# Folding the second batch's keys three slots later, with two issue points per slot, and building one expert's weight forms a step later

## The chip, the cores and the metric

The kernel runs on one core of a Trainium2 chip. The metric is device time in microseconds (us), the median of several executions. PE is the matrix engine (TensorE), DVE the vector engine, ACT the scalar engine, Pool the engine that issues the casting loads, SP the one that issues stores and DMA transposes. Differences here are below one per cent, so every kernel of the experiments was timed in five rounds beside the kernel before, unless a section says "one look": a single profiled execution.

## The reference, cut to what matters

```
attention, B = 8, H = 8, S = 576, D = 64:
  k_p, v_p = means of k and v over 8 neighbouring rows          # 72 rows a head
  attn = softmax(q k_p^T / sqrt(D));   x = attn v_p
mixture of E = 4 experts over N = 4608 tokens, width 512, hidden 1024:
  out = sum_e p[:, e] * (relu(x w1[e]) w2[e])                   # p: normalised domain_probs
```

## The kernel before

The tokens form nine chunks of 512: one for each batch, and a last one from the 64 left-over rows of each. A *step* is one chunk and one expert: step `s` multiplies by w1 ("up", with ReLU) for its own chunk and expert and by w2 ("down") for those of step `s - 1`. A step has eight *slots*. Steps 0 to 3 are chunk 0 (batch 0), so step 4 needs the attention of batch 1. While steps 2 and 3 run, that attention is threaded between the matmuls by a table of slots:

```python
        return {                                          # second_attention(), before
            19: [lambda: fold_keys(1, lo), lambda: fold_keys(1, hi)],   # DVE
            20: [second_keys],                            # PE transposes, ACT copy
            21: [lambda: second_queries(0)],              # PE transposes, DVE copy
            22: [lambda: second_queries(1)],
            23: [lambda: scores(1, 0)],                   # PE, then exp on ACT
            24: [lambda: scores(1, 1), lambda: fold_values(1, lo)],
            25: [lambda: scores(1, 2), lambda: fold_values(1, hi)],
            26: [lambda: scores(1, 3)],
            27: [lambda: context(1, 0), lambda: turn(1, 0)],   # PE, divide on DVE, DMA transpose
            ...                                           # 28, 29, 30: contexts 1, 2, 3
            31: [loads, lambda: load_v(2), lambda: combine_x(1)],
        }
```

`second_keys`, `second_queries`, `scores` and `context` all use one PSUM tile of two banks, one at a time. `combine_x` builds the *x forms* on DVE, sums of blocks of the transposed x; step 4's third product needs them. A step's up part is two rounds of seven products of blocks, with down matmuls between them:

```python
        product(c, e, j, 1, g, True)      # 4 matmuls of 256 columns each
        r1 = keep(g)                      # ACT
        between(0)                        # 3 down matmuls (512 columns), then the slot's pieces
        product(c, e, j, 2, s, True)
        relu_sum(top[:, :, 0:TH], s, r1)  # DVE
        product(c, e, j, 6, g, False)
        r2 = keep(g)
        between(1)                        # 4 down matmuls
        ...                               # products 5 and 7, r3, a relu_sum
        between(2)                        # 5 down matmuls
        product(c, e, j, 4, g, False)
        ...
        between(3)                        # 4 down matmuls
        product(c, e, j, 3, d, False)
        relu_sum(top[:, :, TH:NT], d, r2)
```

The w1 blocks need four sums for each expert too (*weight forms*, `combine_w1`, four DVE operations, one to a slot). All casting loads go through one queue in this order:

```python
        load_probs()
        load_w1(1)
        load_w1(2)
        load_w2(1)
        load_w1(3)
        load_k(1)
        load_q(1)
        load_v(1)
        load_w2(2)       # w2 of the third expert: first used by step 3's down matmuls
        load_w2(3)
        ...
```

Loads for batch 2 follow in the same queue. Pool runs nothing else, so each is issued as soon as its buffer is free: q once the query transposes are done, v once the folds of the values are done.

The softmax here doesn't subtract the row's maximum and nothing guards it: scores larger than these inputs give would overflow.

## Time and profile before

| | before |
|---|---|
| median time | 539.47 us (538.76 to 540.0, 3 runs) |
| span of the profiled execution | 538.1 us |
| PE busy | 516.0 us, 96% |
| DVE, ACT busy | 58%, 43% |

PE is the bound, and the change removes no work from it. So only its waits matter. The longest by the view of PE's waits (what waited, for whom: total us, times, longest us):

```profile
PE g_ps L569 <- DVE H_sb L622: 6.0, 9, 0.8
PE kpt_ps L272 <- DVE kp L190: 4.8, 2, 3.7
PE g_ps L569 <- DVE xf L558: 1.8, 1, 1.8
...
PE o_ps L653 <- DMA w_bf<-in_moe_w_dram: 0.6, 1, 0.6
PE two L348 <- DVE x_tok L330: 0.5, 1, 0.5
...
PE two L225 <- DVE qT L286: 0.4, 1, 0.4
```

The second line is the wait for batch 1's folded keys. Here is PE's timeline around it (start us, us, engine, line, operation, tiles, shapes, count, idle time before and who ended it). `kpt_ps` are the key transposes, `o_ps` the down matmuls, `g_ps` the products:

```profile
47.99 0.81 PE L653 MATMUL o_ps<-w_bf,H_sb 128*128 128x512 bf16 x3
52.49 0.42 PE L272 MATMUL kpt_ps<-ident,kp 72*128 72x72 bf16 x4 [3.68 <-DVE kp L190]
54.07 0.42 PE L272 MATMUL kpt_ps<-ident,kp 72*128 72x72 bf16 x4 [1.16 <-DVE kp L190]
...
63.81 0.81 PE L653 MATMUL o_ps<-w_bf,H_sb 128*128 128x512 bf16 x3
...
82.90 0.61 PE L569 MATMUL g_ps<-xf,w_bf 128*128 128x256 bf16 x4 [1.76 <-DVE xf L558]
```

The line at 63.81 is step 3's first down matmul, the first use of the third expert's w2. It did not wait: that load was issued at 41.73 and took 18.9 us to land, so it was there at 60.6. DVE began the folds at 50.76, after 2.00 us of waiting for the load of k.

The long wait costs twice. The table by stretches shows the granted clock in the third column from the right (the first two columns are the stretch and its length):

```profile
48.00:53.00 5.00, 1.23 (x9) 0.44 (x6) 2.94 (x7) 0.59 (x1) 0.00 (x0) 0.82 1.36 198
53.00:58.00 5.00, 3.93 (x19) 2.29 (x20) 3.43 (x8) 1.22 (x2) 0.00 (x0) 0.50 1.24 206
58.00:63.00 5.00, 4.57 (x42) 3.01 (x40) 3.71 (x6) 1.18 (x2) 1.84 (x3) 1.00 1.26 194
```

By the clock records of the trace PE had half its clock from 51.17 to 57.99. I call this a half-clock stretch.

### The profile page before, as it was taken

The numbers are of one execution on the slowest core, as the hardware profiler recorded it, in microseconds if no ns is written. First come the engines' busy times: TensorE is split into PE (matmuls) and PEld (weight loads), VectorE is DVE, ScalarE is ACT, GpSimd is POOL, SyncE is SP. The second block draws the span as 40 slices with busy tenths as digits, with TensorE's granted clock in tenths as the row PEclk, the third lists the DMA queues.
The fourth block names the chain that finished last, engine by engine and source line by source line (L and its number), as shares of the span: only waits on it lengthen the run. The fifth ranks groups of instructions, "written<-read, shape, count | busy, mean of one in ns | idle before, by whom it ended". The sixth has DMA issues, their size and how long they took to land.

```text
span 538.1 us, 9237 instructions
## 1 busy us (share of the span) xinstructions
PE 516.0 (96%) x3811; PEld 330.2 (61%) x3811; DVE 310.0 (58%) x560; ACT 230.5 (43%) x371; POOL 46.8 (9%) x66
## 2 busy tenths in 40 slices
PE   8896998899999999999999998999999999999996
PEld 4743565566656666566666665666566666666663
DVE  2435785746854667367826656469456644654454
ACT  3652443463355334633473335533643345334430
POOL 8352100200100000101100002000000000000000
PEclk9999899999999999999999999999999999999999
DMA  9999992943580205916631029331101110011003
GB/s 136 203 204 201 193 125 68 158 65 72 77 155 10 41 12 129 133 30 94 113 68 31 20 66 173 45 68 52 40 12 29 49 42 1 10 40 40 2 0 79
DMA packets 75130, 41.52 MB, mean 77 GB/s; under 512 B 44480, under 2 KB 70464, under 8 KB 75088
## 3 DMA queue, kind: packets, MB, share of 16 engines
q0 software_dynamic: 33744, 22.63, 29.4%
q1 hardware_dynamic: 41344, 18.29, 14.3%
q8 instruction: 30, 0.49, 0.4%
q14 instruction: 12, 0.10, 0.1%
HBM read 45.16 MB, written 9.44 MB: 101 GB/s over the span
## 4 chain that ended last, share of the span: by engine, by line
PE 78%; DVE 10%; DMA 8%; POOL 1%; ACT 1%; issue 1%; DVEq 0%; POOLq 0%
PE o_ps L653 39%; PE g_ps L569 36%; DMA w_bf<-in_moe_w_dram 4%; DMA kraw<-in_k_dram 3%; DVE H_sb L622 2%; DVE acc L667 2%; PE two L225 2%; PE two L348 1%; DVE kraw L181 1%; DVE kp L190 1%; ACT r L618 1%; DVE kraw L183 1%; DVE vraw L181 1%; POOL w_bf L134 1%; DVE vraw L183 0%
## 5 line engine op out<-in xcount | busy, mean ns | idle before, releaser
L653 PE MATMUL o_ps<-w_bf,H_sb 128*128 128x512 bf16 x1152 | 294.4, 380 | 0.6 <-DMA w_bf<-in_moe_w_dram 0.6
L569 PEld LDWEIGHTS <-w_bf 128*128 128x128 bf16 x1904 | 181.5, 98 | 79.8 <-issue 13.6
L622 DVE CUSTOM_DVE_ANT_0 H_sb<-g_ps,r 128x512 bf16<-128x512 f32 x204 | 139.7, 688 | 155.8 <-ACT r L618 88.4
L618 ACT COPY r<-g_ps 128x512 f32<-128x512 f32 x204 | 119.4, 585 | 203.1 <-PE g_ps L569 203.1
L653 PEld LDWEIGHTS <-H_sb 128*128 128x128 bf16 x1152 | 112.9, 98 | 78.6 <-issue 1.3
L569 PE MATMUL g_ps<-xf,w_bf 128*128 128x256 bf16 x1088 | 152.7, 273 | 6.2 <-DVE H_sb L622 4.4
L569 PE MATMUL g_ps<-xT,w_bf 128*128 128x256 bf16 x720 | 99.0, 274 | 1.6 <-DVE H_sb L622 1.6
L667 DVE SCALAR_TENSOR_TENSOR acc<-o_ps,p_all,acc 128x512 f32<-128x512 f32 x108 | 80.5, 745 | 19.6 <-PE o_ps L653 19.6
L639 ACT ACTIVATE H_sb<-g_ps 128x512 bf16<-128x512 f32 x68 | 40.4, 595 | 50.6 <-PE g_ps L569 50.6
L229 ACT ACTIVATE expT<-two 72x1024 bf16<-72x1024 f32 x28 | 28.5, 1018 | 10.7 <-PE two L225 10.7
L664 ACT ACTIVATE acc<-o_ps,p_all 128x512 f32<-128x512 f32 x36 | 24.8, 689 | 6.2 <-PE o_ps L653 6.2
L100 POOL DMA_DIRECT2D q_sb<-in_q_dram x7 | 6.3, 897 | 233.9 <-DMA qT<-q_sb 219.1
L330 DVE TENSOR_TENSOR x_tok<-two,inv 128x512 bf16<-128x512 f32 x32 | 22.1, 692 | 1.1
L348 PEld LDWEIGHTS <-expT 72*128 72x128 bf16 x256 | 12.3, 98 | 8.4 <-DVE x_tok L330 1.0
L329 DVE RECIPROCAL inv<-two 128x8 f32<-128x8 f32 x32 | 6.5, 204 | 14.2 <-PE two L348 11.0
L569 PE MATMUL g_ps<-x_rem,w_bf 128*128 128x256 bf16 x96 | 13.3, 273 | 0.0
L348 PE MATMUL two<-vp,expT 72*128 72x65 bf16 x224 | 11.9, 194 | 0.5 <-DVE x_tok L330 0.5
L134 POOL DMA_DIRECT2D w_bf<-in_moe_w_dram x16 | 11.5, 726 | 9.3 <-DMA w_bf<-in_moe_w_dram 9.2
L225 PE MATMUL two<-qT,kpT 64*72 64x256 bf16 x112 | 11.5, 283 | 0.4 <-DVE qT L286 0.4
L225 PEld LDWEIGHTS <-kpT 64*72 64x72 bf16 x112 | 4.1, 107 | 12.3 <-issue 12.3
L181 DVE TENSOR_TENSOR kraw<-kraw 72x1024 bf16<-72x1024 bf16 x14 | 9.5, 678 | 2.0 <-DMA kraw<-in_k_dram 2.0
L181 DVE TENSOR_TENSOR vraw<-vraw 72x1024 bf16<-72x1024 bf16 x14 | 9.5, 678 | 0.0
(82 smaller groups left out, 172.7 us busy)
## 6 DMA issues: line engine op xcount, KB each, us to landing
out_dram<-acc SPq DMA_DIRECT2D x32, 256.0 KB, 2.4
w_bf<-in_moe_w_dram POOLq DMA_DIRECT2D x16, 256.0 KB, 9.9
w_bf<-in_moe_w_dram POOLq DMA_DIRECT2D x4, 1024.0 KB, 16.8
kraw<-in_k_dram POOLq DMA_DIRECT2D x7, 576.0 KB, 9.5
vraw<-in_v_dram POOLq DMA_DIRECT2D x7, 576.0 KB, 11.4
q_sb<-in_q_dram POOLq DMA_DIRECT2D x7, 512.0 KB, 6.2
out_dram<-acc SPq DMA_DIRECT2D x8, 128.0 KB, 2.3
H_sb<-in_k_dram POOLq DMA_DIRECT2D x2, 288.0 KB, 4.5
```

What stands on the lines that cost most here:

```text
L181: nc.vector.tensor_add(out=raw[:, hs, 0:4, :], in0=raw[:, hs, 0:4, :], in1=raw[:, hs, 4:8, :])
L225: nc.tensor.matmul(two[0:SP, r2].rearrange("j (h r p) -> j h r p", h=2, r=2)[:, hh], lhsT=kpT[lo:lo + D, h, 0:SP], rhs=qT[lo:lo + D, h],)
L229: nc.scalar.activation(out=state[("expT", b)][:, 2 * pair:2 * pair + 2].rearrange("j h r s p -> j s (h r) p"), in_=two[0:SP].rearrange("j ...
L330: nc.vector.tensor_tensor(out=x_tok[:], in0=c_ps[:, :, :, 0:D], in1=inv[:].unsqueeze(3).to_broadcast([P, 2, NPAIR, D]), op=ALU.mult,)
L348: nc.tensor.matmul(bank[:, i * (D + 1):(i + 1) * (D + 1)], lhsT=expT[:, h, r // 2, r % 2, :], rhs=vp[:, h, :],)
L569: nc.tensor.matmul(bank[:, t, :], lhsT=w1_bf[:, e, block, kc, lo:lo + P], rhs=x[:, kc, :], start=(first and t == 0 and kc == 0), stop=(t = ...
L618: nc.scalar.copy(out=r[:], in_=ps[:])
L622: nc.vector._custom_dve(TENSOR_ADD_SAT, out=out, in0=ps[:], in1=r[:], s0=BIG, s1=0.0)
L639: nc.scalar.activation(out=low[:, :, 0:TH], in_=g[:], func=ACT.Relu)
L653: nc.tensor.matmul(sums[r][:], lhsT=hidden[(c, e)][:, fc, r * P:(r + 1) * P], rhs=w2_bf[:, e, fc, :], start=(fc == 0), stop=(fc == FCH - 1),)
L664: nc.scalar.activation(out=accs[(c, r)][:], in_=o_ps[:], func=ACT.Copy, scale=prob)
L667: nc.vector.scalar_tensor_tensor(out=dst, in0=o_ps[:], scalar=prob, in1=dst, op0=ALU.mult, op1=ALU.add,)
```

## The change

The intent is to fold the keys when their load has landed, so that DVE does not stand and hold up PE, to place pieces more finely, and to take four weight forms out of the stretch where DVE is busiest. Now each `between` has two issue points, one before and one after its down matmuls, so point 44 is the start of slot 22 and point 47 the end of slot 23.

```diff
-            19: [lambda: fold_keys(1, lo), lambda: fold_keys(1, hi)],
-            20: [second_keys],
-            21: [lambda: second_queries(0)],
-            22: [lambda: second_queries(1)],
-            23: [lambda: scores(1, 0)],
-            24: [lambda: scores(1, 1), lambda: fold_values(1, lo)],
-            25: [lambda: scores(1, 2), lambda: fold_values(1, hi)],
-            26: [lambda: scores(1, 3)],
-            27: [lambda: context(1, 0), lambda: turn(1, 0)],
...                              # 28 to 30: contexts 1 to 3; 31: loads
+            44: [lambda: fold_keys(1, lo)],
+            46: [lambda: fold_keys(1, hi)],
+            47: [second_keys],
+            48: [lambda: second_queries(0)],
+            49: [lambda: second_queries(1)],
+            51: [lambda: scores(1, 0), lambda: fold_values(1, lo)],
+            53: [lambda: scores(1, 1)],
+            55: [lambda: scores(1, 2), lambda: fold_values(1, hi)],
+            57: [lambda: scores(1, 3)],
+            59: [lambda: context(1, 0), lambda: turn(1, 0)],
+            60: [lambda: context(1, 1), lambda: turn(1, 1)],
+            61: [lambda: context(1, 2), lambda: turn(1, 2)],
+            62: [lambda: context(1, 3), lambda: turn(1, 3)],
+            63: [loads, lambda: load_v(2), lambda: combine_x(1)],
...
             def between(j, n):
+                point()
                 if s > 0:
                     down(*steps[s - 1], j, n)
                 slot()          # calls point() too
...
-            elif s == 3:
+            elif s == 4:
                 forms_due.extend(combine_w1(1))
```

More of the change, by code (lines that the diff above doesn't have):

```diff
@@ L475, in second_attention @@
         return {
-            19: [lambda: fold_keys(1, lo), lambda: fold_keys(1, hi)],
-            20: [second_keys],
-            21: [lambda: second_queries(0)],
-            22: [lambda: second_queries(1)],
-            23: [lambda: scores(1, 0)],
-            24: [lambda: scores(1, 1), lambda: fold_values(1, lo)],
-            25: [lambda: scores(1, 2), lambda: fold_values(1, hi)],
-            26: [lambda: scores(1, 3)],
-            27: [lambda: context(1, 0), lambda: turn(1, 0)],
-            28: [lambda: context(1, 1), lambda: turn(1, 1)],
-            29: [lambda: context(1, 2), lambda: turn(1, 2)],
-            30: [lambda: context(1, 3), lambda: turn(1, 3)],
-            31: [loads, lambda: load_v(2), lambda: combine_x(1)],
+            44: [lambda: fold_keys(1, lo)],
[12 more added lines that the diff above has]
+            63: [loads, lambda: load_v(2), lambda: combine_x(1)],
         }
@@ L728, with point @@
         at = 0
-        def slot():
-            nonlocal due, at
-            if forms_due:
-                forms_due.popleft()()
+        def point():
+            nonlocal at
             for piece in placed.pop(at, ()):
@@ L736, in slot @@
             at += 1
+        def slot():
+            nonlocal due
+            if forms_due:
+                forms_due.popleft()()
+            point()
             due += per_slot
@@ L760, in between @@
             def between(j, n):
+                point()
                 if s > 0:
```

## The prediction

> **What bounds the kernel now.** TensorE. The page has PE busy 516.0 of 538.1 us (96%) at a mean granted clock of 0.99; DVE 58%, ACT 43%. The change removes no work: it can only win PE's waits and half-clock time. By PE's waits and timeline, those in reach lie between 48 and 83 us:
>
> - 48.7 to 54.3: PE waits for batch 1's pooled keys (3.68 + 1.16 us <- DVE kp). DVE itself had stood 2.00 us for the load of k, issued at 34.16 and landed at 50.74.
> - After it the clock is halved: the table by stretches has granted clock 0.82 in 48-53, 0.50 in 53-58, 1.00 after. The Trainium skill, "TensorE: Matmul & The Clock Gate", Part 1, says an idle window of about 3.4 us sets the half rate and a busy one lifts it; the trace agrees (about 6.8 us at half). I estimate 1.8 us lost.
> - 62.6 (0.43), 73.2 (0.51), 82.9 (1.76, PE waits for the x forms, they for the last transpose of x, 2.42 us).
>
> In all some 9 us, 1.7%: 2% is out of reach.
>
> **What the change does.** PE, DVE and ACT keep their instructions in another order; POOL's and SP's order is unchanged. Folds move from the end of slot 19 to the starts of slots 22 and 23. By then k has landed. Four forms (0.68 us each) leave step 3, where DVE is 96% busy (63-73), for step 4 (4 us idle in 83-93).
>
> **What it does not win (estimates from the durations above).**
> 1. At full clock PE reaches the first fold's place at about 51.3 and the key transposes at 53.6. Only 2.4 us of matmuls lie between. DVE must do relu-sum, fold (1.59), merge (0.66), form (0.60), fold (1.59) from about 52.1: done near 57.2. PE waits again, about 0.8 + 2.6 us.
> 2. The second wait may halve the clock again (I give it 55%), costing about 2 us.
> 3. Step 3's first down matmul needs w2 of expert 2: issued at 41.73, 18.9 us to landing, so 60.6. Before, PE came at 63.8 and never waited; now it comes near 58.8 and waits 1-2 us. This caps the gain here at 3.2 us.
> 4. The four contexts now stand half a slot apart with one two-bank PSUM tile between them. Each divide costs 0.9 us plus hand-over, with relu-sums between: PE waits about 0.3 + 0.75 + 0.8 us.
> 5. The last x transpose is issued only some 1.6 us earlier than before (near 77.8, was 79.4); the wait for the x forms stays 1.5-2 us.
>
> So PE resumes after the x forms at about 81.3 without the half clock (was 82.9), 83.4 with it. Step 4's forms fill idle DVE time; from chunk 2 on nothing changes. Net: -1.6 or +0.5 us; I lean a little lower, as DVE may reach the folds sooner.
>
> **Predicted:** 538.2 us, 8 in 10 between 535.8 and 540.6; faster by over 2%: 0.01, within 2%: 0.98, slower by over 2%: 0.01.
>
> **What would show it.** PE's wait <- DVE kp 3-4 us instead of 4.8; a new PE wait <- DMA w of 1-2 us near 60; DVE's wait for the k load gone; PE waits for x_tok grown from 0.5 to about 1.5-2 us; PE's wait for xf still 1-2 us.
>
> **What would make it wrong.** w2 landing earlier; DVE not behind at the folds, keys coming at 54-55; a longer half-clock time; x's transposes queueing behind v's next load.

## The result, and the profile after

| | before | after |
|---|---|---|
| median time | 539.44 us (538.76 to 540.0, 4 runs) | 540.5 us (540.32 to 541.4, 4 runs) |
| ratio | | 1.0024, 95% interval 1.0006 to 1.0041 |
| span of the profiled execution | 538.1 us | 538.5 us |

A ratio is the mean time of one kernel's runs over that of the other's of the same rounds, so it is not quite the ratio of the medians. The change costs about one microsecond: the same time by a 2% criterion, but a small loss clear of noise. (The profiled execution of before, 540.12 us, was one of its slower ones, so the two profiles differ by less than the medians.)

The view of PE's waits, after. Line numbers are one higher from the second half of the program on:

```profile
PE kpt_ps L272 <- DVE kp L190: 3.1, 2, 2.5
PE two L348 <- DVE x_tok L330: 1.4, 3, 0.6
...
PE g_ps L570 <- DMA xT<-x_tok: 1.0, 1, 1.0
...
PE g_ps L570 <- DVE xf L559: 0.5, 1, 0.5
...
PE o_ps L654 <- DMA w_bf<-in_moe_w_dram: 0.3, 1, 0.3
```

PE's timeline after, the lines that answer to those of before and the new waits:

```profile
54.97 0.30 PE L272 MATMUL kpt_ps<-ident,kp 72*128 72x72 bf16 x4 [0.60 <-DVE kp L190]
57.81 0.42 PE L272 MATMUL kpt_ps<-ident,kp 72*128 72x72 bf16 x4 [2.54 <-DVE kp L190]
...
61.11 0.59 PE L654 MATMUL o_ps<-w_bf,H_sb 128*128 128x512 bf16 x1 [0.33 <-DMA w_bf<-in_moe_w_dram]
...
74.80 0.43 PE L348 MATMUL two<-vp,expT 72*128 72x65 bf16 x8 [0.16 <-DVE x_tok L330]
...
76.88 0.43 PE L348 MATMUL two<-vp,expT 72*128 72x65 bf16 x8 [0.58 <-DVE x_tok L330]
...
78.38 0.43 PE L348 MATMUL two<-vp,expT 72*128 72x65 bf16 x8 [0.63 <-DVE x_tok L330]
...
81.13 0.61 PE L570 MATMUL g_ps<-xT,w_bf 128*128 128x256 bf16 x4 [1.01 <-DMA xT<-x_tok]
...
83.30 0.61 PE L570 MATMUL g_ps<-xf,w_bf 128*128 128x256 bf16 x4 [0.48 <-DVE xf L559]
```

And the table by stretches, after:

```profile
48.00:53.00 5.00, 5.00 (x36) 3.34 (x35) 4.10 (x8) 1.76 (x3) 0.00 (x0) 1.00 1.57 178
53.00:58.00 5.00, 1.86 (x17) 0.97 (x16) 4.86 (x12) 0.60 (x1) 0.00 (x0) 0.86 1.26 202
58.00:63.00 5.00, 4.46 (x29) 3.15 (x28) 2.39 (x4) 1.22 (x2) 0.00 (x0) 0.50 1.29 204
```

What this says. Between 48 and 53 PE now works at full clock without a gap, as intended. But the wait for the keys has only moved, so that it now begins at 54.4 and not at 48.8: DVE is busy 4.86 of the 5 us from 53 to 58, with the folds, a merge and a weight form between them. It is DVE's own work that PE waits for now, no longer the load. The half clock moved with it (56.59 to 63.42 by the clock records). And PE comes to step 3's first down matmul at 61.11, on the heels of its w2, which landed at 61.1 (issued at 42.17, 18.9 us).

So that matmul starts 2.70 us earlier than before, and yet step 4 goes on after its x forms 0.40 us later (83.30 against 82.90). The stretch between them grew by 3.10 us (from 19.09 to 22.19). From the lines of both traces:

- the second query transposes and the first scores stand after that matmul now (0.45 and 0.34 us before): 0.8 us;
- the waits for the contexts' divides grew from 0.51 to 1.37: 0.86 us;
- the half clock reaches 2.31 us into the stretch, half of which is lost: 1.16 us;
- the waits for transposed x and the x forms: 1.01 + 0.48 for 1.76, so 0.27 us less;
- a gap of 0.22 us inside the first down matmuls.

That is 2.77 of 3.10 us; 0.33 us is spread over gaps too small for me to name. One difference of the two profiles is not among them: after has a half-clock stretch in the startup (19.05 to 22.46) that before lacks. It is no rival for the loss: the two further looks at the changed kernel below lack it too, and step 4 goes on no earlier there. These are sums, not yet causes. The next section takes the suspects away one at a time.

### The profile page after: what moved, and what is told of

Same layout as the page of the kernel before. It is cut to its first block, busy times and chain, and to the rows that moved or that the text cites. A ratio compares the mean times of both kernels' runs of the same rounds, so it can differ in the third digit from the quotient of the medians.

```text
span 538.5 us, 9171 instructions
## 1 busy us (share of the span) xinstructions
PE 514.2 (95%) x3745; PEld 330.9 (61%) x3811; DVE 310.1 (58%) x560; ACT 230.5 (43%) x371; POOL 46.7 (9%) x66
## 4 chain that ended last, share of the span: by engine, by line
PE 77%; DMA 9%; DVE 9%; POOL 2%; issue 1%; ACT 1%; DVEq 0%; POOLq 0%
PE o_ps L654 38%; PE g_ps L570 36%; DMA w_bf<-in_moe_w_dram 9%; DVE H_sb L623 2%; PE two L225 2%; DVE acc L668 2%; PE two L348 1%; POOL w_bf L134 1%; DVE kraw L181 1%; DVE kp L190 1%; ACT r L619 1%; DVE kraw L183 1%; DVE vraw L181 1%; DVE vraw L183 0%; DMA xT<-x_tok 0%
## 5 line engine op out<-in xcount | busy, mean ns | idle before, releaser
L654 PE MATMUL o_ps<-w_bf,H_sb 128*128 128x512 bf16 x1089 | 282.0, 379 | 3.7 <-DMA w_bf<-in_moe_w_dram 0.3
L601 PE MATMUL h_ps<-xT,w_bf 128*128 128x256 bf16 x64 | 9.1, 304 | 0.5 <-ACT xT L385 0.4
```

Of the source, the lines that this page charges most:

```text
L654: nc.tensor.matmul(sums[r][:], lhsT=hidden[(c, e)][:, fc, r * P:(r + 1) * P], rhs=w2_bf[:, e, fc, :], start=(fc == 0), stop=(fc == FCH - 1),)
```

## The experiments

The theories. **H1**: a second half-clock stretch ate the gain. **W**: the landing of the third expert's w2 near 61 holds step 3, so PE can't profit from coming earlier. **L**: v's load for batch 2, issued when the folds of the values are done, now runs while the x transposes want to land. **S**: the half-slot spacing of the contexts sets the tail whatever else happens. **B**: the place of the weight forms matters.

### The weight forms, undone and alone

```diff
# forms_back: from the changed kernel
-            elif s == 4:
+            elif s == 3:
                 forms_due.extend(combine_w1(1))
# forms_only: from the kernel before, the opposite
```

> The changed kernel with the second expert's four forms back in step 3 (one part undone). Theory A (the forms' place hardly matters, since PE's tail wait in step 4 is set by the last context and its transpose): 540.5 us like the changed kernel, within 0.5 us. Rival B (the move of the forms is worth something because DVE is 96% busy in step 3): the contexts' divides come later, PE waits for x_tok and for the x forms grow by 1 to 2 us together, 541.5 to 542.5 us.

> The kernel before with only the forms moved to step 4. Theory A: 539.4 us as before, within 0.5 us; the x forms' wait of 1.76 us stays because it hangs on the last context's place and a 2.4 us transpose. Rival B (DVE load in step 3 holds the contexts back): the 0.51 us wait for x_tok goes and the 1.76 us wait falls by up to 0.6 us; 538.3 to 538.9 us.

Measured: forms_back 540.7 us, 1.003 of before (interval 1.0011 to 1.005), the changed kernel being at 1.0024. forms_only 539.5 us, 1.0005 (0.9986 to 1.0023). In forms_only the 0.51 us wait for x_tok is gone, as B expected, but PE's wait for the x forms stays at 1.76 us, as A expected, and no time is won. B is out: the forms' place is worth nothing that can be measured here.

### Filling PE's waits for the keys

PE is given matmuls on zeros where it waits for the keys anyway, so that it isn't idle. The result is unchanged.

```diff
+        warm(3)                                # before_fill: 17
         for h in range(H):
+            if h == H // 2:
+                warm(11)                       # before_fill: 5
             nc.tensor.transpose(kpt_ps[:, h, :], kps[1][0:SP, h], ident[:SP, :SP])
```

> The changed kernel with 3 + 11 idle-filling matmuls on zeros before the first and the fifth key transpose, where PE waits anyway (0.60 and 2.54 us): PE does not idle there, so the clock should stay full from 48 to 63. Theory H1 (a second half-clock stretch ate the gain): about 2 us faster than the changed kernel, near 538.5 us, with a longer wait for the second expert's... third w2 load (1 to 2 us near 61). Rival H2 (the tail, contexts half a slot apart plus the x transposes behind v's load, sets when step 4 can go on): the clock is full but the time stays at 540 to 540.5 us, and the waits for x_tok, x transposes and x forms grow by what was won.

> The kernel before with 17 + 5 idle-filling matmuls on zeros in its two waits for the keys (3.68 and 1.16 us). H1: no half-clock stretch at 51 to 58, 1.5 to 2 us faster than before, near 537.6 us. H2: the clock is full but the wait for the x forms at 83 grows by as much, 539.4 us.

Measured: before_fill 537.31 us, 0.997 (0.9955 to 0.9985); after_fill 540.29 us, 1.0016 (1.0000 to 1.0032). Both looks have full clock from 48 to 63. So the half-clock stretch cost the kernel before about 2 us, and filling its waits wins them: that version already beats both kernels. The same fill wins nothing in the changed kernel, so H1 alone is not the reason. PE's waits in after_fill say where the time went:

```profile
PE g_ps L573 <- DMA xT<-x_tok: 3.0, 1, 3.0
PE o_ps L657 <- DMA w_bf<-in_moe_w_dram: 1.6, 1, 1.6
PE two L351 <- DVE x_tok L333: 1.4, 3, 0.6
```

What the clock gave came back as a wait for w2 (0.33 to 1.56 us) and for the transposed x (1.01 to 2.98 us).

### Holding v's load of batch 2, and loading w2 earlier

after_fill_hold makes Pool wait for the last x form before it issues that load. after_fill_hold_w2 also swaps two loads.

```diff
+        def hold():
+            nc.gpsimd.tensor_copy(out=held[:], in_=forms[1][3][1][:, 0, 0:1])
-            63: [loads, lambda: load_v(2), lambda: combine_x(1)],
+            63: [loads, lambda: combine_x(1), hold, lambda: load_v(2)],
# the swap, in the ..._w2 kernels
-        load_v(1)
         load_w2(2)
+        load_v(1)
```

> The changed kernel with filled key waits, and v's load for batch 2 held on the Pool queue until batch 1's x forms are done (a one-element copy that reads the last form stands before it). Theory L (in the changed kernel this load, issued near 70.6 and landed near 80.8, runs while the x transposes want to land, which makes step 4 wait): the transposes land 2.4 us after issue, PE's wait of 2.98 us for the transposed x goes to 0, the wait for the x forms stays near 1.5 us: about 2 us faster than the filled changed kernel, near 538.3 us. Rival S (the half-slot spacing of the contexts alone sets the tail): no change, 540.3 us.

> The same, and the w2 load of the third expert is issued before v's load of batch 1. Theory W (the landing of w2 near 61 holds step 3 by 1.56 us): it lands near 58, the wait goes, and 1 to 1.5 us are won on top: near 537 us. Rival: the wait moves on to the queries' copies or to the contexts, no change against the held kernel (538.3 us if L holds).

> Control: the kernel before with filled key waits and v's load for batch 2 held in the same way. Theory L says nothing is won, as there the load has drained before the last transpose (2.42 us from issue): 537.3 us, within 0.5 us. If the hold itself wins or costs something, it shows here.

Measured: after_fill_hold 540.38 us, 1.0018 (0.9999 to 1.0036); after_fill_hold_w2 536.95 us, 0.9963 (0.9948 to 0.9978); the control before_fill_hold 538.09 us, 0.9985 (0.9968 to 1.0002), 0.8 us above before_fill where at most 0.5 was expected, with overlapping intervals. So the hold wins nothing there, and a cost of up to that size can't be excluded.

From after_fill_hold to after_fill_hold_w2 the intervals do not overlap, so with fill and hold in place the swap wins clear of noise, as W says. S is out as the sole cause: PE's waits for the contexts are the same in both looks (0.15, 0.57 to 0.58, 0.62 to 0.63 us), and yet 3.4 us are won. What the spacing costs beside the rest (0.86 us in the list above) no run isolates. And with all three obstacles removed the new schedule is not shown to beat the old one with filled waits: the intervals of after_fill_hold_w2 and before_fill overlap.

In the look at after_fill_hold theory L holds. The view of the transposed x tile gives the least, median and greatest time from issue to landing of its four DMA transposes, in after_fill and then in after_fill_hold:

```profile
DMA to landing us min/median/max: 4.2/5.7/7.7
```

```profile
DMA to landing us min/median/max: 2.4/2.5/2.5
```

With the load in flight (issued at 70.58, 10.2 us to landing) the transposes take up to 7.7 us, without it 2.5 at most. PE's wait for the transposed x goes from 2.98 us to none. The Trainium skill, "DMA: Bandwidth & Descriptors", section "Issuing engines are not separate DMA queues", says that transfers started by different engines run on the same 16 DMA engines and interleave. That agrees with what is seen; the delay is this trace's number.

But the median did not fall, although that look has a span of 537.3 us against 539.1 of after_fill: six executions spread from 536.5 to 539.2. With w2 loaded earlier five executions lie between 534.9 and 535.8. Something about w2's landing made the held kernel uneven. This was left open and is taken up below.

### The swap without the fill, without the hold, and in the kernel before

> The changed kernel with nothing but the order of two loads swapped: w2 of the third expert before v of batch 1. Theory W (w2's landing, different from execution to execution, holds step 3 of the changed kernel): 1.5 to 3 us faster than the changed kernel, 537.5 to 539 us, and less scatter; the half-clock stretch near 57 to 63 stays and still costs about 2 us against the filled one. Rival C (without the filled waits the half clock alone holds step 3): 540 us or more.

> The changed kernel with filled key waits and the two loads swapped, without the hold on v's load of batch 2. Theory L (that load delays the x transposes): PE again waits 2 to 3 us for the transposed x at the start of step 4 and the time is 538.5 to 540 us, 1.5 us or more above the held one (536.95 us). Rival: the hold is worth nothing by itself (as it was without the swap), 537 us.

> Control: the kernel before with the same two loads swapped. Theory W: PE comes to that w2 at 63.8, after its landing in either order, so nothing is won: 539.4 us, within 0.5 us. Rival (the swap is good by itself): 1.5 us or more faster.

Measured: after_w2 539.5 us, 1.0006 (0.9985 to 1.0026); after_fill_w2 537.91 us, 0.9975 (0.9963 to 0.9987); before_w2 538.18 us, 0.9981 (0.9968 to 0.9994).

after_w2 misses its range, and its interval overlaps that of the changed kernel, so the swap alone is not shown to win. It behaves like two kernels in one. Its three executions with a mean granted clock of 0.995 or more took 537.87, 538.39 and 538.61 us; the three with 0.994 or less took 540.38, 540.64 and 541.62. The means are 2.6 us apart. The profiled one is of the first kind: the same waits for the keys (0.59 and 2.54 us) and yet no half-clock stretch there. So the same two waits do or don't halve the clock. That this decides the time in the slower three is likely by their mean clock, but they were not profiled. The Trainium skill, "TensorE: Matmul & The Clock Gate", Part 1, calls the window of 3413 ns in which PE's activity is judged free-running; that fits, and the half-clock stretches of all traces are 3.41 or 6.83 us long, but for those that reach the end of the program.

The traces show what differs. Lay windows of 3.41 us end to end through a trace, so that its half-clock stretches begin and end on their borders. Here is the window before the stretch in the profile of the changed kernel, and then the one that holds most of the same waits in after_w2. PE is busy for 1.49 us in the first (0.44 of it) and for 1.71 us in the second (0.50):

```profile
53.18:56.59 3.41, 1.49 (x11) 0.61 (x9) 3.34 (x8) 0.60 (x1) 0.00 (x0) 1.00 1.27 201
```

```profile
52.90:56.32 3.42, 1.71 (x13) 0.80 (x11) 3.35 (x8) 0.60 (x1) 0.00 (x0) 1.00 1.25 204
```

From 40 us on, in all 20 traces, each of the 25 windows at full clock with PE busy for 0.45 or less (15 of them as the program ends) was followed by half clock, and none with 0.46 or more was. It is not the whole rule: in the startup, near 15 us, windows with 0.54 to 0.61 were followed by half clock too.

after_fill_w2 against after_fill_hold_w2 (537.91 and 536.95 us) leaves about 1 us for the hold, less than the 1.5 us expected and not clear of noise, as the intervals overlap. So L is shown by the looks and not by the medians; PE waits 1.51 us for the transposed x there.

before_w2 contradicts me: nothing was to be won, and about 0.2% was, clear of noise by its interval. In its look w2 is not waited for, as in that of before, and the waits for the keys are about the same (3.36 and 1.16 us). But that look is the slowest of the five executions (539.8 us), so it shows least of the gain. I can't name the source.

### Another order of loads under the kernel before

```diff
# before_fill_kfirst: before_fill with 8 + 5 filling matmuls, the swap above, and
+        load_k(1)
         load_w1(3)
-        load_k(1)
```

> The kernel before with filled key waits (8 + 5 matmuls), k's load of batch 1 issued before the fourth expert's w1, and w2 of the third expert before v's load. If the folds in slot 19 wait for the load (landed 50.74, DVE ready at 48.8), the load lands near 46 and 1.5 to 2 us are won on top of the filled one: near 535.6 us. Rival: DVE's own folds (2 times 1.6 us from 48.8) set the keys, or the queries (landed near 54) do: less than 0.7 us won, 536.6 to 537.3 us.

Measured: 537.76 us, 0.9975 (0.9957 to 0.9993), nothing won over before_fill and above both forecasts. k landed at 44.1 and the keys came with a wait of 0.20 us, but PE then waited 1.61 us for the transposed x at the start of step 4, a wait that before_fill does not have. v's load of batch 2 had been issued at 66.17 and landed at 77.9. This is the collision of theory L again, now under the other schedule: being earlier at the keys brings the transposes into the load. The queries' landing (53.0) may have played a part too, as the rival said; this run does not part the two.

### A version built from what was found

ahead loads k before the fourth expert's w1, w2 before v, and holds v of batch 2. Its table of points:

```diff
+            40: [lambda: fold_keys(1, lo)],
+            42: [lambda: fold_keys(1, hi)],
             47: [second_keys],
+            48: [lambda: second_queries(0), lambda: warm(6), lambda: second_queries(1)],
+            49: [lambda: scores(1, 0)],
+            51: [lambda: scores(1, 1)],
+            53: [lambda: scores(1, 2), lambda: fold_values(1, lo)],
+            55: [lambda: scores(1, 3), lambda: fold_values(1, hi)],
+            57: [lambda: context(1, 0), lambda: turn(1, 0)],
+            59: [lambda: context(1, 1), lambda: turn(1, 1)],
+            60: [lambda: context(1, 2), lambda: turn(1, 2)],
+            61: [lambda: context(1, 3), lambda: turn(1, 3)],
...
-                forms_due.extend(combine_w1(0) + combine_w1(3))
+                forms_due.extend(combine_w1(0) + nothing[:2] + combine_w1(3))
```

> A version built from what the runs showed: k of batch 1 loaded before the fourth expert's w1, w2 of the third expert before v, v of batch 2 held; folds in slots 20 and 21, where DVE gets two slots without weight forms; keys where the changed kernel has them; both query transposes before step 3's first down matmul with 6 filling matmuls between; scores and contexts one to two points earlier. If loads and DVE's order are what holds this stretch: no wait for the keys, no half clock, PE at step 3's first down matmul near 58, 534.5 to 536 us. If the divides or the x transposes set the tail regardless, 537 us like the held and swapped one.

Measured: 535.82 us (535.09 to 536.36), 0.9934 of before (0.9922 to 0.9946), the best version and correct. It changes the loads, the folds' places, the fill and the spacing at once, so this run does not say which of them wins how much. PE does not wait for the keys at all. Its timeline, from the key transposes to the x forms:

```profile
53.16 0.43 PE L272 MATMUL kpt_ps<-ident,kp 72*128 72x72 bf16 x8
...
57.46 0.81 PE L656 MATMUL o_ps<-w_bf,H_sb 128*128 128x512 bf16 x3
...
72.85 0.43 PE L348 MATMUL two<-vp,expT 72*128 72x65 bf16 x8 [0.58 <-DVE x_tok L330]
...
77.83 0.61 PE L572 MATMUL g_ps<-xf,w_bf 128*128 128x256 bf16 x4 [0.74 <-DVE xf L561]
```

Step 3's first down matmul starts at 57.46 and step 4 goes on at 77.83, against 61.11 and 83.30 in the changed kernel. Clock is full from 48 to 83.

### A dose of w2, and what the slow executions have

The two late-w2 kernels exchange the last two weight loads, so that the third expert's w2 lands about 5 us later. The looks repeat kernels unaltered.

```diff
# after_fill_w2late, before_fill_w2late
+        load_w2(3)
         load_w2(2)
-        load_w2(3)
```

> The filled changed kernel with the w2 loads of the third and fourth expert exchanged, so that the third's lands near 66 instead of 61. If its landing gates step 3 here: PE waits about 6.5 us for it instead of 1.56, the time is 3 to 5 us longer (span 542 to 544 us). If not, no change.

> The filled kernel before with the same exchange. PE comes to that w2 at about 62 there, so it should wait about 4 us where it waited none, the tail's waits take up to 1 us of it back: 3 to 4 us longer (span 538.5 to 540 us). The dose-response is then steeper in the changed kernel by the 1.56 us that it already waits.

> The changed kernel unaltered, another look. If the second half-clock stretch is usual, it is there again (about 6.8 us at half from 56 to 63) and the span is 538.3 to 538.7 us; if an execution without it comes, about 2 us less in the key stretch but longer waits for w2 or for the transposed x.

> The filled and held changed kernel unaltered, another look. If w2's landing scatters, a slow execution (539 us span) has it near 62.5 instead of 60.9 and PE's wait for it near 3 us. Rival: another wait (transposes, startup) is longer by 1.5 us and w2 lands at 60.4 to 61.3 as in all eight looks so far.

> If this look falls on a slow execution (span near 539 us), the longer wait shows between 40 and 83 us, by w2's landing (rival: by the startup). If it is another 537.1 to 537.3 us one, the cause stays open.

> The changed kernel, a third look: half clock from about 57 to 64 again if the waits for the keys (0.60 and 2.54 us) set it in most phases of the clock's window, span 538.3 to 538.7 us.

Measured, one look each. after_fill_w2late: PE waits 6.12 us for w2, span 543.7 us. before_fill_w2late: 3.58 us, span 541.6 us. So w2's landing gates both kernels once it is late enough, and the changed one at its usual time already. The size of the dose was off: step 4 goes on 4.65 us later than in after_fill and 4.76 us later than in before_fill, no steeper in the changed kernel, and the span of before_fill_w2late is above its range. Both looks have a half-clock stretch after the long wait (62.73 to 69.56, and 66.63 to 70.04), which I had not reckoned with.

The looks at the held kernel settle what was open. First look1, with a span of 537.1 us like the first profile, then look2, with 538.8 us one of the slow kind:

```profile
58.23 0.30 PE L275 MATMUL kpt_ps<-ident,kp 72*128 72x72 bf16 x4 [0.16 <-DVE kp L190]
...
60.81 0.81 PE L660 MATMUL o_ps<-w_bf,H_sb 128*128 128x512 bf16 x3 [0.95 <-DMA w_bf<-in_moe_w_dram]
61.46 0.61 PE L285 MATMUL qt_ps<-ident,q_sb 128*128 128x128 bf16 x8
```

```profile
56.69 0.30 PE L275 MATMUL kpt_ps<-ident,kp 72*128 72x72 bf16 x4 [0.16 <-DVE kp L190]
...
60.86 0.81 PE L660 MATMUL o_ps<-w_bf,H_sb 128*128 128x512 bf16 x3 [2.54 <-DMA w_bf<-in_moe_w_dram]
61.51 0.95 PE L285 MATMUL qt_ps<-ident,q_sb 128*128 128x128 bf16 x8
```

w2 lands at the same time in both (60.8). But in look2 PE came 1.5 us sooner: look1 had a half-clock stretch in the startup (19.26 to 22.67), look2 had none. Coming sooner, it waits 2.54 us in place of 0.95, that idle time halves the clock from 61.62 to 65.03, and step 4 goes on at 83.61 in place of 81.89. The table by stretches of look2 shows it:

```profile
58.00:61.00 3.00, 0.46 (x7) 0.30 (x5) 1.09 (x2) 0.49 (x1) 0.00 (x0) 1.00 1.25 208
61.00:63.00 2.00, 2.00 (x15) 1.50 (x14) 0.50 (x1) 0.00 (x0) 0.23 (x1) 0.65 1.27 178
63.00:65.00 2.00, 2.00 (x9) 1.11 (x8) 1.70 (x4) 0.59 (x1) 2.00 (x3) 0.50 1.06 119
```

My expectation had the sides reversed: not the landing scatters but PE's arrival, and the sooner it comes, the later it gets away. The landing itself was at 60.1 to 61.3 in every look with the original order of loads.

The further looks at the changed kernel: spans 538.6 and 539.1 us, half clock from 57.73 to 64.56 and from 58.00 to 64.83, waits for w2 of 0.93 and 2.57 us. With the first profile that is a half-clock stretch of 6.83 us here in three looks of three. By the mean granted clock of the four timed executions, three have 0.990 and one, the slowest, 0.997; what that one had instead was not profiled. (From these means I estimate about 10.8 us at half clock in the three, and 3.2 us in the slowest, which leaves no room for a stretch of 6.83 us.)

All looks that matter, side by side (us from the start; the last column is the difference):

| look | w2 landed | step 3's first down matmul | step 4 goes on after the x forms | between |
|---|---|---|---|---|
| before | 60.6 | 63.81 | 82.90 | 19.09 |
| after | 61.1 | 61.11 | 83.30 | 22.19 |
| after, looks 1 and 2 | 60.1, 60.9 | 60.13, 60.96 | 83.35, 83.90 | 23.22, 22.94 |
| after_fill | 60.9 | 60.99 | 83.84 | 22.85 |
| after_fill_hold, first look and look1 | 60.8, 60.8 | 60.88, 60.81 | 81.96, 81.89 | 21.08, 21.08 |
| after_fill_hold, look2 | 60.8 | 60.86 | 83.61 | 22.75 |
| after_fill_hold_w2 | 57.7 | 59.11 | 80.52 | 21.41 |
| ahead | 57.0 | 57.46 | 77.83 | 20.37 |

In every row with the original order of loads, the changed schedule starts that matmul within 0.1 us of w2's landing. After it, a half-clock stretch (after, look2 of the held kernel) or the transposes behind v's load (after_fill) take 1.1 to 2.1 us over the clean 21.08. And the clean 21.08 is still 1.99 us longer than the 19.09 of before; the moved pieces and the contexts' waits of the list above make up 1.66 of it.

## Why the prediction was right or wrong, point by point

It was wrong in its net: 538.2 us and a gain were forecast, 540.5 us and a loss of 0.24% were measured. The time lies inside the range (535.8 to 540.6), near its upper end, and the class "within 2%" is right.

- *The keys' wait, "about 0.8 + 2.6 us", with DVE done "near 57.2".* Right: 0.60 and 2.54 us, done at 57.8, in a trace whose PE came about 0.6 us later to this place.
- *The w2 load as a cap, "lands at 60.6", "waits 1-2 us".* Right in kind: the first down matmul starts with the landing, at 60.1 to 61.1, in all three looks. The wait was 0.33, 0.93 and 2.57 us.
- *The contexts, "about 0.3 + 0.75 + 0.8 us".* Measured 0.16, 0.58 and 0.63 us, a fifth to a half below the forecast.
- *The x forms' wait of 1.5 to 2 us.* Right in the further looks: 1.47 and 1.66 us, and no wait for the transposed x. In the first profile it is 1.49 us in sum, but by luck: 1.01 of it was a wait for the transposed x itself, which the prediction only listed among what could go wrong ("x's transposes queueing behind v's next load"). In the filled kernel, holding that load took this wait away.
- *The forms in step 4 fill idle DVE time.* Right: moving them wins and costs nothing that these runs can measure.
- *The failing step: "The second wait may halve the clock again (I give it 55%)", and then "Net: -1.6 or +0.5 us; I lean a little lower, as DVE may reach the folds sooner."* The branch with the half clock was computed as 83.4 for step 4 going on; the three looks gave 83.30, 83.35 and 83.90. So the size of that branch was right. What failed is the weighing of the two, and the good branch itself. The half clock was the usual case: five of the six executions seen have it (three timed ones by their mean clock, the profile among them, and both looks). A window of 3.41 us slid along the trace of after_w2, which has these two waits at full clock, holds 0.45 or less of PE work in 83% of its phases (an estimate from that one trace). Nothing supported the lean: DVE reached the folds when reckoned. And the good branch (81.3) was not to be had: with full clock through this stretch, after_fill went on at 83.84, and the one timed execution of the changed kernel whose mean clock leaves no room for the long half-clock stretch was the slowest (541.4 us). The runs show what the prediction lacked: the terms are coupled. An execution that escapes one loss and comes earlier runs into the fixed landing of w2, idles there, and has its clock halved for that (look2 of the held kernel), or brings the x transposes into v's load (after_fill). Both were seen in the filled variants; for the changed kernel itself they are inferred. I had treated the half clock as a coin toss on one wait and the w2 landing as a plain cap.
- *The loss itself.* The branch of +0.5 us was the profiles' difference (+0.4 us). The medians differ by 1.06 us; the traces do not show the remaining half microsecond, as the profiled execution of before was a slow one.

Still open: why swapping the two loads wins 0.2% in the kernel before, where no look shows a wait for them; what the slowest timed execution of the changed kernel had, at a mean clock of 0.997; what the contexts' spacing costs by itself; and 0.33 us of the list above.

## What to carry to other kernels

When a stretch is held by several things of nearly the same time (a load's landing, an engine's queue, a transpose), removing the first wait mostly exposes the next: list the landing times first, and change the order of the loads before the order of the compute. A wait of PE can cost once more in half clock (after one of 2.54 us, the held kernel went on 1.72 us later than its other look); whether it does depends on how much PE works in the clock's window around it. So where a wait is unavoidable, matmuls on zeros in it are worth trying (here 2 us in the kernel before). A load that is issued as soon as its buffer is free follows the compute that frees it, so moving that compute moves the load, perhaps into a latency-critical transfer.

## What the Trainium skill lacked or had wrong

- "TensorE: Matmul & The Clock Gate", Part 1, has the half rate set after at least one idle window of about 3.4 us. Here less was enough: one wait of 2.54 us was followed by a half-clock stretch of 3.41 us (look2 of the held kernel), and waits of 0.60 and 2.54 us by one of 6.83 us. The page gives no share of the window that counts as idle, not even where it tells of short, frequent idle times. Here, from 40 us on, windows with PE busy for 0.45 or less were followed by half clock and those with 0.46 or more were not. It tells of the free-running window for the warm-up; that the same two waits halve the clock in one trace (after) and not in another (after_w2), by where they fall in the window, it does not say.
- "DMA: Bandwidth & Descriptors" says that all transfers interleave on the same engines, and in "Rules for kernel authors" that a transpose next to ordinary DMAs "needs nothing". For correctness the runs agree. For time it lacks the cost: 2.4 to 2.5 us from issue to landing with v's load held (after_fill_hold), 4.2 to 7.7 us beside that 576 KB casting load (after_fill).
